# Row-halved scores and outer products, gate weights applied off TensorE, and written-out orders in a fused linear-attention and expert-attention kernel

## The chip, the cores and the metric

The kernel runs on one core of one Trainium2 chip. The metric is the device time of one execution in microseconds, the median of several runs. Engines are named as in the profile: PE (TensorE matmul), PEld (its weight loads), DVE (VectorE), ACT (ScalarE), POOL (GpSimd), SP (the queue that issues most transfers).

## The reference

Two layers, one after the other. The first is linear attention with a norm for each head; the second is attention with four experts, of which each token takes two.

```python
q, k, v: (8, 8, 576, 64)                       # batch, heads, tokens, head size
kv  = einsum('bhsd,bhse->bhde', k, v)
out = einsum('bhsd,bhde->bhse', q, kv)
x   = out / sqrt(mean(out*out, -1) + 1e-6) * g_norm   # heads side by side: (8, 576, 512)

logits = x @ w_gate                            # 4 experts
w      = softmax over the two largest, 0 for the others
for e in range(4):                             # wq, wk, wv: (4, 512, 64)
    q, k, v = x @ wq[e], x @ wk[e], x @ wv[e]
    a   = causal softmax(q @ k.T / 8)
    y  += w[:, e] * (a @ v @ wo[e])            # wo: (4, 64, 512)
```

## The kernel before

The work is cut by batch (b = 0 to 7) and by blocks of 128 tokens (i = 0 to 4, the last has 64). For a batch the stages are, with the names that the profile shows for their PSUM tiles:

- `kv` (L607, p_kv): for each pair of heads, k transposed times v, f32. Two heads write the two column halves of one PSUM bank. `kvx_copy` puts the result into `kvx` as a block-diagonal matrix: head one in partitions 0 to 63, head two in 64 to 127, zeros elsewhere.
- `kt` and `kg` (L641, L651): kv is transposed on PE and multiplied with the gate weights, which lie block-diagonal in `wg_bd`. The four products a head go beside kv in `kvx` (68 columns a head), so the next stage gives the gate logits as well.
- q transposed: on PE for the first two batches (L625), on DVE for the others (L633).
- `out_mm` (L670, p_out): for each of four pairs of heads one f32 product over all 128 partitions with 136 columns. The profile counts two instructions for each f32 product.
- `sq_act` (ACT), `red` (DVE), then `newton`: eleven small DVE operations on 128 x 40 numbers give one over the root. `xm` (L751, POOL) multiplies; `x_tr` transposes x on PE (L625, p_x).
- gates: `gl`, `lg`, `m8`, `sh` (L776), `ex`, `mk`, `gt`, `den`, `rd`, `gate`, nearly all on DVE.
- `v_mm` (L811), `proj` for q and k (L829), in fp32r, for two pairs of experts (pr = 0, 1).
- `sc` (L858, p_sc): the scores of two experts. k transposed lies in two tiles, one an expert, in which the other expert's 64 partitions are zero. So each product runs over all 128 partitions of q. Its 12 products a pass stream 512, 64, 448, 320, 192 and 64 columns for each of the two experts. `exp` (L872, ACT), `msk` (POOL, the causal triangle), `pv` (L892), then a scale by gate over sum on DVE, `ot` (L936) and `y_mm` (L948), copies and stores.

The order is not that of the loops. `graph` lists every task with its engine, an assumed duration and what it needs; `plan` simulates the engines and takes, at each step, the ready task with the smallest due time, which `urgency` computes from a table. `SWAP` moves single PSUM copies between ACT and DVE. PSUM has two small slots (one bank each) and three large ones (two banks each). Each engine works through its queue strictly in the resulting order.

Loads come in through SP, those of batch 0 in part through ACT's queue: `lg0` issues eight small transfers there (norm and gate weights), before ACT's table load and its first copy. PE's `keep_warm` issues nothing here, since `WARM` is 0.

Of the kernel before, what the change touches and what calls it, by code (L numbers as in the profile page):

```python
# [10 lines left out]
FP32 = mybir.dt.float32  # L11
FP32R = mybir.dt.float32r
BF16 = mybir.dt.bfloat16
I32 = mybir.dt.int32
# [3 lines left out]
NB, NCH, EP = 5, 4, 2  # L18
QPE = 2
# [4 lines left out]
LOADS = ("lk", "lv", "lkr", "lvr", "lq", "lg0", "lw", "lwo", "st")  # L24

SWAP = {
    "ws": (('q', 0), ('v', 0),), "qc": ((0, 4), (1, 0), (1, 1), (1, 3),),
    "oc": ((0, 0), (0, 1), (1, 2), (1, 3), (1, 4), (6, 1), (6, 2), (6, 3), (7, 2), (7, 3),),  # L30
    "xc": ((0, 0), (0, 1), (1, 0), (1, 2), (1, 4), (6, 0), (6, 2), (6, 3), (7, 2), (7, 4),),
    "vc": ((0, 0), (6, 0), (6, 1), (6, 2),), "qpc": ((0, 0), (1, 0), (7, 0), (7, 1),),
    "kpc": ((0, 0), (6, 0), (7, 0),), "otc": ((0, 1), (1, 0), (1, 1), (6, 0), (6, 1),),
    "yc": ((0, 1), (0, 4), (1, 0), (1, 1), (1, 2), (1, 3), (1, 4), (6, 2), (6, 3),), "kvx": ((1,), (6,), (7,),),
    "kvc": ((1,),), "ktc": ((7,),),
}


def swapped(n):
    return n[1:] in SWAP.get(n[0], ())  # L40


def earlier(n, m):

    return len(n) > 1 and isinstance(n[1], int) and n[1] < m[1]


def graph(B):
    t = {}

    def add(name, eng, hold, lat, needs=(), tiles=()):
        t[name] = (eng, hold, lat, [n for n in needs if n in t], list(tiles))

    def pe(name, hold, needs, tiles=()):
        add(name, "PE", hold, hold + 0.27, needs, tiles)

    def act(name, took, needs, tiles=()):
        add(name, "ACT", took - 0.10, took + 0.06, needs, tiles)

    def dve(name, took, needs, tiles=()):  # L60
        add(name, "DVE", took - 0.05, took + 0.05, needs, tiles)

    def pool(name, took, needs, tiles=()):
        add(name, "POOL", took - 0.03, took + 0.10, needs, tiles)

    def copy(name, on_act, on_dve, needs, tiles=(), first=dve):

        ways = ((dve, on_dve), (act, on_act))
        if first is act:
            ways = ways[::-1]  # L70
        make, took = ways[swapped(name)]
        make(name, took, needs, tiles)

    R5, R4, R2 = range(NB), range(NCH), range(EP)
    for b in range(B):

        q2 = "ACT" if b == 0 else "SP"
        for p in R4 if b == 0 else R2:
            lat = 0.92 if b == 0 else 1.84
            add(("lk", b, p), "SP", 0.55, lat, (), (("k", b),))  # L80
            add(("lv", b, p), q2, 0.55, lat, (), (("v", b),))
        add(("lkr", b), "SP", 0.65, 0.67, [("kv", b - 2, c) for c in R4])
        add(("lvr", b), q2, 0.65, 0.67, [("kv", b - 2, c) for c in R4])
        for i in R5 if b < QPE else range(8):
            lat = (1.32 if i < NF else 0.66) if b < QPE else 1.06
            add(("lq", b, i), q2 if i % 2 else "SP", 0.6, lat, (), (("q", b),))
        if b == 0:
            add(("lg0",), "ACT", LG0, 0.3)
            dve(("wg",), 0.85, [("lg0",)])
            for nm in "qkv":  # L90
                for p in R2:
                    add(("lw", nm, p), "SP", 0.55, 0.92, (), (("x", nm, p),))
                    name, nd = ("ws", nm, p), [("lw", nm, p), ("lg0",)]
                    (dve if swapped(name) else pool)(name, 0.60 if swapped(name) else 1.08, nd, (("x", nm, p),))
            for p in R2:
                add(("lwo", "o", p), "SP", 0.55, 0.84, (), (("y", "wo", p),))
                dve(("wo", "o", p), 0.42, [("lwo", "o", p)], (("y", "wo", p),))

        for c in R4:
            pieces = (c,) if b == 0 else (c // 2,) if b < QPE else R2  # L100
            nd = [(m, b, p) for m in ("lk", "lv") for p in pieces] + [("lkr", b), ("lvr", b)]
            pe(("kv", b, c), 0.76, nd, (("sm", "kv", b), ("k", b), ("v", b)))
        copy(("kvx", b), 0.76, 0.84, [("kv", b, c) for c in R4] + [("out", b - 2, i) for i in R5], (("sm", "kv", b),))
        copy(("kvc", b), 0.37, 0.43, [("kvx", b), ("kt", b - 2)], (("sm", "kv", b),), act)
        for i in R5:
            if b < QPE:
                last = i == NF
                pe(("q", b, i), 0.38 if last else 0.44, [("lq", b, i)], (("sm", "q", b, i), ("q", b)))
                copy(
                    ("qc", b, i), 0.37 if last else 0.59, 0.42 if last else 0.69, [("q", b, i), ("out", b - 1, i), ("out", b - 1, NF)],  # L110
                    (("sm", "q", b, i),),
                )
            elif i < NCH:
                nd = [("lq", b, i // 2 * 4 + r) for r in R4] + [("out", b - 1, j) for j in R5]
                dve(("qc", b, i), 0.80, nd, (("q", b),))
        pe(("kt", b), 0.20, [("kvc", b)], (("sm", "kt", b),))
        copy(("ktc", b), 0.37, 0.42, [("kt", b)], (("sm", "kt", b), ("kvT", b)))
        pe(("kg", b), 0.42, [("ktc", b), ("wg",)], (("sm", "kg", b), ("kvT", b)))
        copy(("kgc", b), 0.44, 0.34, [("kg", b)] + [("out", b - 2, i) for i in R5], (("sm", "kg", b),))
        for i in R5:  # L120
            pe(
                ("out", b, i), 0.95, [("qc", b, j) for j in ((i, 0) if b < QPE else R4)] + [("kvx", b), ("kgc", b)],
                (("bg", "out", b, i),),
            )
            copy(
                ("oc", b, i), 0.66, 0.73, [("out", b, i), ("xm", b - 1, i), ("gl", b - 1), ("sq", b - 1, i)],
                (("bg", "out", b, i),),
            )
            n = NB * b + i - 3
            act(("sq", b, i), 0.60, [("oc", b, i), ("red", n // NB, n % NB)])  # L130
            dve(("red", b, i), 0.69, [("sq", b, i), ("nw", b - 2, 10)])
        for j in range(11):
            dve(("nw", b, j), 0.19, [("red", b, i) for i in R5] if j == 0 else [("nw", b, j - 1)])
        dve(("gl", b), 0.33, [("nw", b, 10)], (("gl", b),))
        dve(("lg", b), 0.43, [("gl", b), ("mk", b - 2), ("sh", b - 2)], (("gl", b),))
        for i in R5:
            pool(("xm", b, i), 1.08, [("nw", b, 10)], (("x", b, i),))
        for i in R5:
            last = i == NF
            pe(("x", b, i), 0.38 if last else 0.44, [("xm", b, i)], (("sm", "x", b, i), ("x", b, i)))  # L140
# [72 lines left out]
    return t  # L213


NF = 4
LG0 = 5.0
WARM = 0.0
COLD = 6.005
# [787 lines left out]
```

The softmax here doesn't subtract the row's maximum and nothing guards it: scores larger than these inputs give would overflow.

## Time and profile before

| what | value |
|---|---|
| time, median of 3 runs | 254.58 us (253.85 to 255.46) |
| profiled execution, first to last instruction | 250.9 us |
| PE, PEld busy | 221.2 us (88%), 199.0 us (79%) |
| DVE busy | 180.0 us (72%), 510 instructions |
| ACT busy | 148.8 us (59%), 258 instructions |
| POOL busy | 81.1 us (32%), 159 instructions |
| moved by DMA | 40.28 MB, mean 161 GB/s |

The span is that of one execution. The median of the runs lies 3.7 us above it; that part is outside the first and the last instruction. Busy time is a union: two overlapping instructions of an engine count once, so the sum of the durations of a group is larger than what it adds to busy time. Matmuls overlap most. PE's pace is therefore read from the chain of waits, in which each step is counted from the end of the one before, and not from the mean duration of an instruction. Most starving is at both ends: PE is busy 3.79 us between 10 and 20 us, and 20.46 of the last 25.90 us.

### The profile page before, as it was taken

What the parts mean: (1) busy time and instruction counts of PE and PEld (TensorE: products, weight loads), DVE (VectorE), ACT (ScalarE), POOL (GpSimd) and SP (SyncE); (2) the same over time, 40 slices, a digit from 0 to 9 for tenths busy, and PEclk for the clock granted to TensorE, in tenths of its full rate; (3) what the DMA queues carried; (4) which work ended last, traced back from release to release, by engine and by line L of the source; (5) the groups of instructions that cost most, each with busy time, mean ns of one, the idle gap of its engine ahead of it and who ended that gap; (6) DMA issues with size and microseconds to landing.
All of it is one profiled execution on the core that took longest, in us unless ns stands there. A gap on an engine that the chain in (4) does not pass through costs nothing.

```text
span 250.9 us, 6366 instructions
## 1 busy us (share of the span) xinstructions
PE 221.2 (88%) x2456; PEld 199.0 (79%) x2456; DVE 180.0 (72%) x510; ACT 148.8 (59%) x258; POOL 81.1 (32%) x159
## 2 busy tenths in 40 slices
PE   0726957999999999999999998989999699999982
PEld 0714847999999879996998988979988699888850
DVE  0084698688898978998699928976878887794560
ACT  0003450664923976359738993488899556838973
POOL 8300016604800256006700920066006600902310
PEclk9999995999999999999999999999999899999998
DMA  6997999999999989895999993021034100104245
GB/s 172 302 163 223 288 243 283 231 135 285 189 161 332 136 165 343 120 240 184 247 129 272 220 167 103 3 86 42 3 123 173 42 0 3 43 3 146 79 156 189
DMA packets 99433, 40.28 MB, mean 161 GB/s; under 512 B 76618, under 2 KB 94538, under 8 KB 99402
## 3 DMA queue, kind: packets, MB, share of 16 engines
q1 hardware_dynamic: 94320, 38.15, 65.8%
q10 hardware_dynamic: 5082, 1.72, 3.2%
q8 instruction: 19, 0.31, 0.6%
q14 instruction: 12, 0.10, 0.2%
HBM read 30.43 MB, written 9.44 MB: 159 GB/s over the span
## 4 chain that ended last, share of the span: by engine, by line
PE 71%; DVE 11%; DMA 7%; ACT 7%; issue 1%; SPq 1%; ACTq 0%; DVEq 0%
PE p_out L670 13%; PE p_sc L858 9%; PE p_v L811 8%; PE p_k L829 7%; PE p_q L829 7%; PE p_kv L607 6%; PE p_x L625 6%; PE p_y L948 6%; PE p_pv L892 6%; DMA q_b<-in_q_dram 3%; ACT PT L872 3%; DMA k_b<-in_k_dram 3%; DVE sh L776 2%; PE p_q L625 2%; PE p_ot L936 1%
## 5 line engine op out<-in xcount | busy, mean ns | idle before, releaser
L878 POOL TENSOR_SCALAR_AFFINE_SELECT PT<-PT 128x256 bf16<-128x256 bf16 (+1 forms) x80 | 29.0, 383 | 102.0 <-ACT PT L872 87.0
L751 POOL TENSOR_TENSOR x_tok<-o_sb,rs 128x512 f32<-128x512 f32 (+1 forms) x40 | 41.6, 1121 | 54.0 <-DVE rs L725 51.5
L872 ACT ACTIVATE PT<-p_sc 128x128 bf16<-128x128 f32 (+1 forms) x64 | 51.4, 849 | 6.9 <-PE p_sc L858 6.5
L670 PE MATMUL p_out<-kvx,qT 128*128 128x136 f32 x320 | 44.8, 290 | 0.7 <-DVE kvx L493 0.5
L670 PEld LDWEIGHTS p_out<-kvx,qT 128*128 128x128 f32 x320 | 41.9, 199 | 1.4 <-DVE kvx L493 0.5
L858 PE MATMUL p_sc<-qTp,kT 128*128 128x64 f32 (+4 forms) x192 | 39.8, 335 | 0.6 <-ACT PT L872 0.4
L690 ACT ACTIVATE sq<-o_sb 128x512 f32<-128x512 f32 (+1 forms) x40 | 25.3, 637 | 19.2 <-DVE o_sb L493 16.8
L858 PEld LDWEIGHTS p_sc<-qTp,kT 128*128 128x128 f32 x192 | 28.5, 190 | 4.4 <-ACT PT L872 1.1
L696 DVE TENSOR_REDUCE ms<-sq 128x8 f32<-128x520 f32 (+1 forms) x40 | 27.2, 682 | 5.8 <-ACT sq L690 5.5
L493 DVE COPY o_sb<-p_out 128x544 f32<-128x544 f32 (+1 forms) x30 | 21.6, 719 | 13.3 <-PE p_out L670 12.8
L607 PE MATMUL p_kv<-v_b,k_b 128*64 128x64 f32 x512 | 21.7, 236 | 7.6 <-DMA k_b<-in_k_dram 7.5
L811 PE MATMUL p_v<-wv_r,xT 128*128 128x256 f32 x160 | 26.6, 296 | 0.9 <-DVE vext L493 0.7
L625 PE MATMUL p_x<-ident_f,x_tok 128*128 128x128 f32 (+1 forms) x160 | 23.4, 279 | 3.9 <-DVE mk L785 2.2
L607 PEld LDWEIGHTS p_kv<-v_b,k_b 128*64 128x64 f32 x512 | 19.3, 148 | 9.4 <-DMA v_b<-in_v_dram 7.3
L948 PE MATMUL p_y<-wo_b,OT 128*128 128x512 bf16 x80 | 22.7, 381 | 1.0 <-ACT xT L491 0.7
L811 PEld LDWEIGHTS p_v<-wv_r,xT 128*128 128x128 f32 x160 | 21.6, 189 | 2.2 <-DVE vext L493 1.0
L625 PEld LDWEIGHTS p_x<-ident_f,x_tok 128*128 128x128 f32 (+1 forms) x160 | 17.9, 146 | 6.2 <-issue 3.2
L491 ACT CAST xT<-p_x 128x512 fp32r<-128x512 f32 (+1 forms) x30 | 15.7, 546 | 10.6 <-PE p_x L625 10.5
L829 PE MATMUL p_k<-xT,wk_r 128*128 128x288 f32 x128 | 20.2, 301 | 0.0
L491 ACT COPY y<-p_y 128x512 f32<-128x512 f32 (+1 forms) x31 | 17.8, 593 | 3.8 <-PE p_y L948 2.6
L829 PE MATMUL p_q<-xT,wq_r 128*128 128x288 f32 x128 | 19.1, 299 | 0.0
L491 ACT CAST kT<-p_k 64x576 fp32r<-64x576 f32 x26 | 16.5, 634 | 4.2 <-PE p_k L829 4.0
(89 smaller groups left out, 325.1 us busy)
## 6 DMA issues: line engine op xcount, KB each, us to landing
out_dram<-y SPq DMA_DIRECT2D x32, 256.0 KB, 2.2
k_b<-in_k_dram SPq DMA_DIRECT2D x14, 512.0 KB, 5.5
v_b<-in_v_dram SPq DMA_DIRECT2D x14, 512.0 KB, 7.1
q_b<-in_q_dram SPq DMA_DIRECT2D x48, 144.0 KB, 4.8
q_b<-in_q_dram SPq DMA_DIRECT2D x6, 256.0 KB, 8.2
k_rem<-in_k_dram SPq DMA_DIRECT2D x8, 128.0 KB, 3.9
v_b<-in_v_dram ACTq DMA_DIRECT2D x4, 256.0 KB, 6.5
k_b<-in_k_dram SPq DMA_DIRECT2D x4, 256.0 KB, 6.3
```

The source lines that it names most:

```text
L491: nc.scalar.copy(dst, src)
L607: nc.tensor.matmul(p_kv[hh * Dh : (hh + 1) * Dh, c, :], lhsT=lhs, rhs=rhs, start=(j == 0), stop=(j == NF), skip_group_check=True,)
L625: nc.tensor.transpose(p_t[:, c, :nt], chunk(c)[:nt], ident_f[:nt, :nt])
L670: nc.tensor.matmul(p_o[:, c // 2, (c % 2) * 256 : (c % 2) * 256 + 2 * GW], lhsT=blocks_of(qT, c)[:, i * P : (i + 1) * P], rhs=kvx[b % 2][: ...
L696: nc.vector.tensor_reduce(mss[b % 2][:nt, i, :], sqs[(NB * b + i) % 3][:nt], axis=AX_X, op=AluOpType.add)
L751: nc.gpsimd.tensor_tensor(out=buf(("x", b, i), [P, NCH, P], FP32, "x_tok")[:nt].rearrange("p c (h r) -> p h r c", h=H), in0=ob[:nt, i, :, ...
L811: nc.tensor.matmul(p_v[:], lhsT=blocks_of(xTs[b % 2], c)[:, i * P : (i + 1) * P], rhs=w_r["v"][:, c, :, :].rearrange("p e f -> p (e f)"), ...
L829: nc.tensor.matmul(p_p[:, s, 0:HALF], lhsT=w_r[nm][:, c, 2 * pr : 2 * pr + 2, :].rearrange("p e f -> p (e f)"), rhs=blocks_of(xTs[b % 2], ...
L858: nc.tensor.matmul(p_s[:, el, o : o + hi - lo], lhsT=kTs[pr][el][:, kb * P : (kb + 1) * P], rhs=tiles["qTp", b, pr][:, lo:hi], start=True, ...
L872: nc.scalar.activation(PT[:, :, d0 : d0 + o], big("sc", b, pr, j)[:, :, 0:o], ACTF.Exp, scale=scale)
L878: nc.gpsimd.affine_select(out=d, in_=d, compare_op=AluOpType.is_ge, fill=0.0, base=0, pattern=[[0, 2], [1, w]], channel_multiplier=-1,)
L948: nc.tensor.matmul(p_y[:], lhsT=blocks_of(OTs[b % 2], pr)[:, qc * P : (qc + 1) * P], rhs=wo_b[:, pr, :], start=(pr == 0), stop=(pr == EP - 1),
```

## The change

All tasks stay, but for `kt`, `kg` and their copies. What differs:

- **Row halves.** `sc` and `out_mm` now take one head's or expert's 64 partitions on each side. Head 0 uses partitions 0 to 63, head 1 the others, into two PSUM banks, in alternating instructions. The zero-filled k tiles and the block-diagonal `kvx` are gone; k transposed is copied in one piece.
- **Gate weights off PE.** kv is copied to `kvx`, multiplied with spread-out gate weights (`kvg_mul`, DVE or POOL) and summed (`kvg_sum`, DVE).
- **Gate weights spread by PE.** At the start two rows of gate weights are loaded through POOL's queue, and `gb` multiplies them with a row of ones, which puts them on all partitions.
- **Norms.** ACT's Ln and Exp give a first value and three small operations refine it. In batch 0 each block of tokens is normed by itself.
- **Zero matmuls.** PE runs products of zeros ahead of five tasks, 30 of them ahead of `gb`.
- **Orders.** `graph` and `plan` are gone. The order of all tasks, the engine of each elementwise task and the slot of each buffer are written out as strings. 30 of the 40 `xm` products go to DVE, 22 of the 40 squares to POOL. PSUM is four slots of two banks, of which small tiles take halves.
- x is turned by an fp32r product with an identity, and not by a transpose. The last 64-token block of y is computed and stored in two column halves. q loads of the first two batches are split in two and all issued by SP.

```diff
+ZEROS = {
+    ("gb",): 30, ("q", 0, 0): 1, ("q", 0, 2): 2, ("out", 0, 3): 4, ("v", 0, 0): 3,
+}
...
     def lv(b, p):
         load_main(queue(b, True), v_t(b), v, b, p)
+        if (b, p) == (0, NCH - 1):
+            nc.scalar.preload_act_table_set("natural_log_exp_and_others")
...
-    def lg0():
-        nc.scalar.dma_start(g_wide[:], g_norm.unsqueeze(0).to_broadcast([P // Dh, Dh]))
...
+    def gb():
+        p_w = big("gb")
+        for a in range(2):
             for m in range(EP):
-                nc.scalar.dma_start(wg_st[pp, m], by_head[:, 4 * m + 2 * c2 : 4 * m + 2 * c2 + 2, :])
...
+                nc.tensor.matmul(
+                    p_w[a * Dh : (a + 1) * Dh, m, :], lhsT=one_row[0:1, :], rhs=wg_row[a][:, m * 512 : (m + 1) * 512],
+                    start=True, stop=True, skip_group_check=True,
+                )
...
+    def kvg_mul(b, g):
+        ms = of_part(b, g)
+        n = ms.stop - ms.start
+        ew(("kgm", b, g)).tensor_tensor(
+            out=kvgs[b % 2][:].rearrange("p e (m k) d -> p e m (k d)", k=2)[:, :, ms],
+            in0=kvx[b % 2][:, ms, E : E + 2 * Dh].unsqueeze(1).to_broadcast([P, E, n, 2 * Dh]),
+            in1=wg_t[:].rearrange("p e (m k) d -> p e m (k d)", k=2)[:, :, ms], op=AluOpType.mult,
+        )
...
+    def kvg_sum(b, g):
+        ms = of_part(b, g)
+        nc.vector.tensor_reduce(
+            gates_of(kvx[b % 2])[:, ms], kvgs[b % 2][:].rearrange("p e (m k) d -> p m k e d", k=2)[:, ms], axis=AX_X,
+            op=AluOpType.add,
+        )
...
     def out_mm(b, i):
-        p_o = big("out", b, i)
+        p_o, nt = big("out", b, i), blocks[i][1]
         for c in range(NCH):
-            nc.tensor.matmul(
-                p_o[:, c // 2, (c % 2) * 256 : (c % 2) * 256 + 2 * GW],
-                lhsT=blocks_of(qT, c)[:, i * P : (i + 1) * P],
-                rhs=kvx[b % 2][:, c, :, :].rearrange("p a g -> p (a g)"),
-                start=True,
-                stop=True,
-            )
+            for hh in range(2):
+                pp = slice(hh * Dh, (hh + 1) * Dh)
+                nc.tensor.matmul(
+                    p_o[:nt, hh, c * GW : (c + 1) * GW],
+                    lhsT=qTs[b % NQT][pp, c * S + i * P : c * S + i * P + nt],
+                    rhs=kvx[b % 2][pp, c // 2, c % 2 * GW : (c % 2 + 1) * GW],
+                    start=True,
+                    stop=True,
+                )
...
+    def ln(b, g):
+        cols, ms = span(b, g), mss[b % 2][:].rearrange("p n h -> p (n h)")
+        nc.scalar.activation(roots[b % 2][:, cols], ms[:, cols], ACTF.Ln)
+
+    def rs(b, g):
+        cols = span(b, g)
+        nc.scalar.activation(rstds[b % 2][:, cols], roots[b % 2][:, cols], ACTF.Exp, scale=-0.5)
...
     def xm(b, i):
...
-        nc.gpsimd.tensor_tensor(
...
+        ew(("xm", b, i)).tensor_tensor(
...
+    def x_tr(b, i):
+        p_t, nt = small("x", b, i), blocks[i][1]
+        for c in range(NCH):
+            nc.tensor.matmul(
+                p_t[:, c * P : c * P + nt], lhsT=tiles["x", b, i][:, c, :], rhs=ident_r[:, 0:nt], start=True, stop=True
+            )
...
             for el in range(2):
+                pp = slice(el * Hd, (el + 1) * Hd)
                 nc.tensor.matmul(
                     p_s[:, el, o : o + hi - lo],
-                    lhsT=kTs[pr][el][:, kb * P : (kb + 1) * P],
-                    rhs=tiles["qTp", b, pr][:, lo:hi],
+                    lhsT=kTs[(2 * b + pr) % 3][pp, kb * P : (kb + 1) * P],
+                    rhs=tiles["qTp", b, pr][pp, lo:hi],
...
     with tc.manual_schedule():
-        for t, _, n in plan(tasks, POOLS, {n: urgency(n) for n in tasks})[0]:
...
+        for n in order:
+            if n in ZEROS:
+                zero_matmuls(n, ZEROS[n])
             emit[n[0]](*n[1:])
```

## The prediction

> **What bounds the kernel now.** I read the windows by stage first, then the chain of waits, the groups and the wait list. In the windows each engine's busy time stands with its instruction count:
>
> ```profile
> 10.00:20.00 10.00, 3.79 (x44) 3.07 (x44) 5.50 (x13) 1.37 (x2) 0.00 (x0) 1.00 1.03 173
> ...
> 50.00:75.00 25.00, 25.00 (x325) 23.67 (x327) 21.39 (x64) 13.72 (x24) 9.32 (x16) 1.00 1.12 193
> ...
> 175.00:200.00 25.00, 22.84 (x208) 20.16 (x207) 19.94 (x51) 21.50 (x39) 8.61 (x15) 0.97 0.24 86
> ```
>
> Columns: window, length, busy us of PE, PEld, DVE, ACT, POOL, clock, DMA share, GB/s. See three stages: a start of 50 us in which PE starves; 175 us (50 to 225) with PE busy 170.1 us by the sum of the seven windows, 97%; a tail of 26 us. DVE has 142.4 us in the middle, 81%: it is the next limit, not far below. The chain agrees and names the lines:
>
> ```profile
> PE 71%; DVE 11%; DMA 7%; ACT 7%; issue 1%; SPq 1%; ACTq 0%; DVEq 0%
> PE p_out L670 13%; PE p_sc L858 9%; PE p_v L811 8%; PE p_k L829 7%; PE p_q L829 7%; PE p_kv L607 6%; PE p_x L625 6%; PE p_y L948 6%; PE p_pv L892 6%; DMA q_b<-in_q_dram 3%; ACT PT L872 3%; DMA k_b<-in_k_dram 3%; DVE sh L776 2%; PE p_q L625 2%; PE p_ot L936 1%
> ```
>
> PE's pace, first from the chain in order of time, then from the timelines of PE and of the weight loads (start, us, what):
>
> ```profile
> 130.33 0.93 PE p_out L670 x8
> ...
> 132.92 2.48 PE p_kv L607 x80
> ...
> 236.15 1.37 PE p_sc L858 x10
> ```
>
> ```profile
> 131.62 1.30 PE L829 MATMUL p_k<-xT,wk_r 128*128 128x288 f32 x8
> 132.85 0.69 PE L607 MATMUL p_kv<-v_b,k_b 128*64 128x64 f32 x16
> ...
> 139.25 0.54 PEld L651 LDWEIGHTS p_kg<-wg_bd,kvT 128*128 128x128 f32 x4
> ...
> 139.59 0.19 PEld L651 LDWEIGHTS p_kg<-wg_bd,kvT 128*128 128x128 f32 x1
> ```
>
> The kg matmuls stream only 16 columns, yet their loads start (139.59 - 139.25)/3 = 0.113 us apart: a full f32 load takes that long. The kv instructions load 64 columns and write alternate column halves; 2.48/80 = 0.031 us each is about half of 0.113/2, so two halves work at once. And k's eight, at 1.06/8 = 0.132, would let the next begin at 132.68; kv begins at 132.85, so entering the halved mode cost 0.17.
>
> The start and the stalls, from the wait list, the chain and a group:
>
> ```profile
> ACT L428 <- DMA wg_st<-in_moe_w_gate_dram: 18.6, 1, 18.6
> ...
> PEld p_q L625 <- ACT kvc L491: 5.8, 1, 5.8
> ```
>
> ```profile
> 10.06 7.89 DMA q_b<-in_q_dram
> ...
> 193.06 3.93 DVE sh L776
> ```
>
> ```profile
> L751 POOL TENSOR_TENSOR x_tok<-o_sb,rs 128x512 f32<-128x512 f32 (+1 forms) x40 | 41.6, 1121 | 54.0 <-DVE rs L725 51.5
> ```
>
> ACT issues eight gate-weight and norm loads up to 19.5 us; its first copy (kvc) comes after them, and PE waits. The sh line is a 20-element subtraction that took 3.93 us while POOL ran five x_tok products.
>
> [...]
>
> **PE, part by part.** Pair prices are the larger of a load (0.113) and a stream (0.46 ns a column from 0.119 for v's 256).
> - Scores: now 12 a pass, ten at 1.37 and the two of 512 at 0.22 (y's 0.88/4), 1.81 us. Afterwards six pairs: 64, 64 and 192 columns at 0.113, then 0.147, 0.206 and 0.22: 0.91. Sixteen passes: 29.0 to 14.6, **-14.4**.
> - out: 8 instructions of 0.116 (0.93) become 16 with a load each; two at a time 16 x 0.113/2 = 0.90, and half for the 64-token tile. 40 x 0.93 = 37.2 becomes 32 x 0.90 + 8 x 0.45 = 32.4: **-4.8**.
> - kt and kg off PE: six loads of 0.113 a batch, 0.68 x 8: **-5.4**. Last y block in column halves: 8 x 0.22: **-1.8**.
> - x by fp32r product instead of transpose: load-bound on both sides (0.105 now): 0. [...]
> - Mode changes: the PE order has 72 stretches of one mode against 20: 52 x 0.17 = **+8.8** (0 to 15).
>
> Sum -17.6 of 203 (now kv 19.8, q 4.3, kt and kg 5.4, out 37.2, x 17, v 19, k and q 34, scores 29, pv 15.4, ot 4.4, y 17.6), so 25.4 us a batch becomes 23.2. These edits are charged wholly to PE, which is the path; about 0.85 of them, -15, fall in the middle stage.
>
> **DVE, ACT, POOL, queues.** DVE, by rows of before: Newton 17.5 out, 26 small operations of 0.2 in: -12.3. Thirty x_tok products come from POOL at 0.67 (the weight product L584): +20.1. kv times gate weights: products 5 x 1.2 + 2 x 0.67, sums 7 x 1.25 + 2 x 0.68 (scaled from 0.685 for 520), less 10.1 of kvx, kvT and kvc copies: +7.5. Most of sh, and parts of gt, gl, gate and inv go to POOL: -15. PSUM copies exchanged with ACT: -5; set-up 0. About -5 on 202 summed: DVE stays near 177 busy while the span shrinks. ACT loses 22 squares (0.64) and the doubled kT copies (26 to 9), gains 24 Ln/Exp (0.24) and vext copies: about -17, off the path. POOL trades 30 x 1.12 for 22 squares of about 1.1 and small work: even. What POOL blocks on DVE is the unknown: 30 products, each meeting half a POOL operation in 0.4 of cases, 0.2 us: +6, from 0 to 15. That puts DVE's share of a middle of 160 us at 144/160, 90%. At 81% PE lost 4.9 us; I take 6 more (0 to 12) as given back. What is late next is a copy out of PSUM behind a product in DVE's queue, and PE waits for that bank. sh's own stalls on the chain (3.9 and 1.7) mostly go: -4. SP issues ten more q loads and eight more stores at 0.6 us, and two q loads that were ACT's; the middle hides them behind data that arrives batches early. In the start they stand before the weight loads. POOL issues four gate and norm loads ahead of its memsets, not on the path.
>
> **The start.** PE first runs 30 zero matmuls, then gb, with kv queued behind both. Zeros: kv's first sixteen took 1.12 us against 0.64 later, so cold is 0.22 x 1.75 = 0.39; [...] 8 us from 1.3 to 9.4. gb: four f32 products of 512 columns, 0.88 each scaled from out: to 12.9. kv warm, 2.5: to 15.4, against 12.9 now. That is 2.5 late. But ACT is free, so copy, product and sum of both parts (2 x 1.6, begun at 14.4) release out(0) at about 17.7, against 26.2 now. Each tile is then normed alone: square, sum, Ln, Exp, three steps and product are about 3.5 us, and ACT's square and copy (1.25 a tile) pace the rest: v(0) ends near 33 against 52.9. Before had by then done kv(1), q(1) and out(1) too, 2.5 + 2.2 + 4.6 = 9.3. Gain 52.9 - 33 - 9.3 = 10.6. Low end 4: the q load landed at 17.95 and may again; high end 14.
>
> **Sum.** Start -10.5; middle -15 for PE, +6 given back to DVE, -4 for sh; tail -1 (the last store chain stays). -24.5 on a span of 250.9 gives 226.4. The median (254.58) lies 3.7 above the profiled span; I add that to every span: **230 us**. Own range 217 to 243.
>
> **Rivals.** (1) DVE takes the bound: 177 + 15 of locks, kept at 90% as an in-order queue, is 213; with 18 us of idle start and 5 of tail, 236 + 3.7 = 240; range 236 to 250. For: 81% already. Against: the worst lock of before leaves. (2) Row halves don't overlap, the slower side: out 32 x 1.81 + 8 x 0.90 = 65.1 (+27.9), scores still 29.0, less 7.2, plus 8.8: PE +29; less 11.5 for start and tail, 272. It decides from where PE grows by 12: the sum is -17.6 + 47.1 g, g the share of pairs that run singly, so g above 0.63. For: only columns are seen overlapping. Against: kv's 0.031. (3) The start is held by data: DMA share is 1.0 up to 150 us, so only 4 of the 10.5 come, and half of the middle's 13: about 243. (4) Overlap without mode cost, and DVE keeping up: 210 to 217.
>
> **Chances.** Forecast 0.63, rivals (1) and (3) together 0.22, (2) 0.07, (4) 0.08. The range takes the forecast, most of (1) and (3) and part of (4): 213 to 246. A measurement here tells about 1% from no change. Faster by over 1%: the forecast, (4) and nearly all of (1) and (3): 0.90; within 1%: 0.04; slower: 0.06.
>
> **What would show it.** Right: sixteen out instructions near 0.9 us, a score pass near 0.9; first out near 18 us, v(0) done near 33; DVE at 80% or more of the span; sh no longer in the chain; one table load. Wrong: out tiles of 1.7 us; a start of 45 us; DVE leading the chain; xm on DVE well over 0.67.

## The result, and the profile after

The changed kernel takes 277.23 us (median of 4 runs, 275.66 to 278.55); the kernel before, run beside it, 254.44 (253.85 to 255.46). The ratio is 1.0909, 95% interval 1.0834 to 1.0984: slower by 9%, where 230 was forecast. The profiled execution took 278.12, with a span of 276.3 and a mean granted clock of 0.873; before it was 250.9 and 0.977. From here on a measured time is the median of the executions within 1.5% of the fastest of their kernel, as in the ratios, and the range is that of all; the expectations quote medians of all.

Windows by stage of the changed kernel (window, length, busy us of PE, PEld, DVE, ACT, POOL, clock, DMA share, GB/s):

```profile
25.00:50.00 25.00, 22.39 (x175) 19.41 (x175) 13.42 (x36) 7.74 (x23) 4.74 (x7) 0.59 0.94 234
50.00:75.00 25.00, 21.20 (x280) 18.94 (x280) 19.91 (x38) 13.06 (x25) 9.70 (x16) 0.89 0.98 184
...
125.00:150.00 25.00, 24.13 (x254) 21.55 (x255) 18.10 (x37) 11.75 (x20) 9.69 (x16) 0.75 0.63 145
...
200.00:225.00 25.00, 21.16 (x253) 18.82 (x250) 19.53 (x36) 12.96 (x23) 13.48 (x20) 0.82 0.14 49
```

Two things are new. PE has gaps (21.20 of 25 where it had 25.00), and the clock column is low in windows where PE is busy: from 25 to 50 only 0.59. In the page's slices the clock row shows how long such spells last; first the row of before (a slice is 6.3 us), then that of the changed kernel (6.9 us):

```profile
PEclk9999995999999999999999999999999899999998
```

```profile
PEclk9998557999599779995599999995999669889998
```

The page's chain of waits, by engine and by line:

```profile
PE 58%; DVE 25%; ACT 4%; issue 4%; DMA 4%; SPq 2%; POOL 0%; ACTq 0%; DVEq 0%; POOLq 0%
PE p L427 10%; PE p L574 10%; PE p L593 9%; DVE x_tok L508 9%; PE p L519 6%; PE p L712 5%; PE p L744 5%; PE p L654 4%; PE p L377 3%; PE p L620 3%; DVE ms L456 2%; DMA q_b<-in_q_dram 2%; DVE xT L270 2%; DMA out_dram<-y 1%; DVE qT L417 1%
```

DVE went from 11% of a span of 251 to 25% of one of 276, from some 28 to 69 us, and about 24 of these (8.5% before rounding) are one line: x_tok (L508), the norm's product. Its group, and the waits that it ends:

```profile
L508 DVE TENSOR_TENSOR x_tok<-o_sb,rstd 128x512 fp32r<-128x512 f32 x30 | 35.5, 1265 | 0.1
```

```profile
PE p L519 <- DVE x_tok L508: 10.5, 12, 2.1
...
PEld p L519 <- DVE x_tok L508: 8.9, 10, 2.3
```

The chain in order of time (start, us, what) shows the clock in single pieces:

```profile
36.67 2.86 PE p L574 x12
...
53.81 1.99 PE p L427 x32
...
71.17 2.93 PE p L574 x12
```

Twelve matmuls of v take 2.86 and 2.93 with the clock column at 0.50 in both stretches; at the pace of before (0.95 for eight) they are 1.43. Two row-halved out tiles, with the column at 1.00, take 1.99, where two whole ones of before took 1.86.

### The profile page after: what moved, and what is told of

The parts are those of the page before. It is cut to its first block, busy times and chain, and to the rows that moved or that the text cites. A ratio compares the mean times of both kernels' runs of the same rounds, so it can differ in the third digit from the quotient of the medians.

```text
span 276.3 us, 6932 instructions
## 1 busy us (share of the span) xinstructions
PE 239.8 (87%) x2792; PEld 202.5 (73%) x2792; DVE 191.3 (69%) x425; ACT 132.2 (48%) x247; POOL 98.5 (36%) x182
## 4 chain that ended last, share of the span: by engine, by line
PE 58%; DVE 25%; ACT 4%; issue 4%; DMA 4%; SPq 2%; POOL 0%; ACTq 0%; DVEq 0%; POOLq 0%
PE p L427 10%; PE p L574 10%; PE p L593 9%; DVE x_tok L508 9%; PE p L519 6%; PE p L712 5%; PE p L744 5%; PE p L654 4%; PE p L377 3%; PE p L620 3%; DVE ms L456 2%; DMA q_b<-in_q_dram 2%; DVE xT L270 2%; DMA out_dram<-y 1%; DVE qT L417 1%
## 5 line engine op out<-in xcount | busy, mean ns | idle before, releaser
L634 ACT ACTIVATE PT<-p 128x1024 bf16<-128x1024 f32 (+1 forms) x64 | 50.8, 840 | 8.0 <-PE p L620 7.6
L427 PE MATMUL p<-kvx,qT 64*128 64x68 f32 (+1 forms) x640 | 40.7, 274 | 3.5 <-DVE o_sb L270 3.4
L427 PEld LDWEIGHTS p<-kvx,qT 64*128 64x128 f32 (+1 forms) x640 | 37.4, 186 | 8.4 <-DVE o_sb L270 3.7
L519 PE MATMUL p<-ident_r,x_tok 128*128 128x128 f32 (+1 forms) x160 | 30.8, 338 | 12.5 <-DVE x_tok L508 10.5
L519 PEld LDWEIGHTS p<-ident_r,x_tok 128*128 128x128 f32 x160 | 27.7, 252 | 16.1 <-DVE x_tok L508 8.9
L574 PE MATMUL p<-wv_r,xT 128*128 128x256 f32 x160 | 35.7, 380 | 1.0 <-ACT xT L268 0.6
L508 DVE TENSOR_TENSOR x_tok<-o_sb,rstd 128x512 fp32r<-128x512 f32 x30 | 35.5, 1265 | 0.1
L574 PEld LDWEIGHTS p<-wv_r,xT 128*128 128x128 f32 x160 | 30.2, 271 | 3.8 <-DVE xT L270 1.1
L452 POOL TENSOR_TENSOR sq<-o_sb 128x512 f32<-128x512 f32 (+1 forms) x22 | 22.7, 1037 | 19.5 <-DVE o_sb L270 11.3
L620 PE MATMUL p<-qTp,kT 64*128 64x64 f32 (+4 forms) x192 | 24.1, 354 | 1.2 <-ACT qTp L268 0.4
## 6 DMA issues: line engine op xcount, KB each, us to landing
out_dram<-y SPq DMA_DIRECT2D x32, 256.0 KB, 2.9
k_b<-in_k_dram SPq DMA_DIRECT2D x4, 256.0 KB, 6.7
v_b<-in_v_dram ACTq DMA_DIRECT2D x4, 256.0 KB, 8.6
```

The source lines that it names most:

```text
L427: nc.tensor.matmul(p_o[:nt, hh, c * GW : (c + 1) * GW], lhsT=qTs[b % NQT][pp, c * S + i * P : c * S + i * P + nt], rhs=kvx[b % 2][pp, c // ...
L508: ew(("xm", b, i)).tensor_tensor(out=buf(("x", b, i), [P, NCH, P], FP32R, "x_tok")[:].rearrange("p c (m k r) -> p m k r c", m=NCH, k=2), i ...
L519: nc.tensor.matmul(p_t[:, c * P : c * P + nt], lhsT=tiles["x", b, i][:, c, :], rhs=ident_r[:, 0:nt], start=True, stop=True)
L574: nc.tensor.matmul(p_v[:, 0 : E * Hd], lhsT=blocks_of(xTs[b % 2], c)[:, i * P : (i + 1) * P], rhs=w_r["v"][:, c, :, :].rearrange("p e f -> ...
L620: nc.tensor.matmul(p_s[:, el, o : o + hi - lo], lhsT=kTs[(2 * b + pr) % 3][pp, kb * P : (kb + 1) * P], rhs=tiles["qTp", b, pr][pp, lo:hi], ...
L634: nc.scalar.activation(PT[:, :, d0 : d0 + o], big("sc", b, pr, j)[:, :, 0:o], ACTF.Exp, scale=scale)
```

## The experiments

**What the x_tok products cost on DVE.** In the timeline of the changed kernel, DVE's products and POOL's instructions beside them (start, us, engine, line):

```profile
62.90 3.79 DVE L508 TENSOR_TENSOR x_tok<-o_sb,rstd 128x512 fp32r<-128x512 f32 x4
...
66.11 2.69 POOL L395 TENSOR_TENSOR kvg<-kvx,wg_t 128x1024 f32<-128x1024 f32 x1 [3.47 <-ACT kvx L268]
...
68.91 1.02 DVE L508 TENSOR_TENSOR x_tok<-o_sb,rstd 128x512 fp32r<-128x512 f32 x1
...
179.82 4.94 DVE L508 TENSOR_TENSOR x_tok<-o_sb,rstd 128x512 fp32r<-128x512 f32 x4
...
179.94 1.84 POOL L508 TENSOR_TENSOR x_tok<-o_sb,rstd 128x512 fp32r<-128x512 f32 x1 [0.21 <-DVE rstd L487]
...
181.65 1.17 POOL L493 TENSOR_TENSOR gl<-o_sb,rstd 128x160 f32<-128x160 f32 x1
```

Four products take 3.79 while POOL is idle but for the last 0.6, some 0.95 each, and 4.94 while POOL works. Between the first four and the fifth DVE has a `gl` of 2.45 beside POOL's kvg, where the other two on DVE took 0.33, and the fifth begins at 68.91, just after kvg's end at 68.80. Such stretches of DVE beside POOL are what the prediction and the expectations call locks; that the one waits for the other is a reading of these times. So the products were moved back to POOL, alone (in `unpack`):

```diff
+    engine.update({n: "G" for n in ns if n[0] == "xm"})
```

> The changed kernel with all 40 x_tok products on POOL. Theory A (thirty products on DVE, 1.02 to 2.16 us each, 35.5 us in all, keep DVE from its copies): DVE busy falls by some 30 us to 160, the time to 255 to 268 us. Theory B (what counts is how late x is, not who computes it: five products in a row on POOL are 5.7 us, against about 4.5 shared): no gain, 275 to 290 us.

Measured: 261.98, 262.51 and 263.89 in three executions and 257.87 in a fourth, against 254.97 before: 13 to 19 of the 22 are gone. The chain of waits by engine and the group of products, of the execution of 262.51:

```profile
PE 64%; DVE 16%; POOL 8%; ACT 5%; issue 4%; DMA 1%; ACTq 0%; DVEq 0%; POOLq 0%
...
L509 POOL TENSOR_TENSOR x_tok<-o_sb,rstd 128x512 fp32r<-128x512 f32 x40 | 42.8, 1132 | 10.9 <-ACT xT L269 6.6
```

POOL's product is no faster (1132 ns), but DVE, now 160.0 busy for 191.3, is free for the copies out of PSUM. The placement of this one step is the largest single cost that was found. How it costs is shown only in part: the clock is higher too, 0.911 against 0.873, and the shorter waits and the better clock were not taken apart.

**The clock.** The same was asked from the other side: three zero matmuls ahead of every x tile of batches 1 to 7, nothing else changed.

```diff
+ZEROS.update({("x", b, i): 3 for b in range(1, 8) for i in range(5)})
```

> The changed kernel with three zero matmuls ahead of each x tile of batches 1 to 7 (105 of 0.22 us, 23 us of PE work that waits for nothing but its PSUM slot). Theory C (PE's waits at x let the granted clock fall to half, and the work after it runs at half pace): mean clock from 0.87 to 0.95 or more, 255 to 268 us, although no wait is removed. If the waits alone are the cost and the clock is a by-product: 277 to 295 us.

Measured: 271.63 (270.1 to 272.54), ratio 1.0676 (1.0613 to 1.0740), clock 0.966. The clock came back as theory C said, the time hardly: it lies between the two forecasts. On the chain of waits the zero matmuls (105 new ones beside 40) grew from 5% to 9% of the span, some 10 us, so they took part of what they restored; and DVE still held 29% of it.

Next, with the products on POOL, the squares went to ACT, where before has them all; then, each on top of that, out in whole-array products, or six zeros ahead of only the first x tile of a batch. The whole-array version leaves out the zeros of the block-diagonal matrix, so it sums two heads and serves for its time alone.

```diff
+    engine.update({n: "G" if n[0] == "xm" else "A" for n in ns if n[0] in ("xm", "sq")})
```

> The changed kernel with all 40 x_tok products on POOL and all 40 squares on ACT, as the kernel before has them. Theory A (the assignment of the norm's steps to engines costs the time: locks between DVE and POOL, and a loaded POOL): POOL falls from 118 busy to about 96, ACT rises from 132 to about 146, and the time falls from 262 (products on POOL alone) to 252-258. Theory C (what is left over is the clock, fed by an order with little cover behind each x tile): 259-264, the clock stays near 0.91. Theory M (what is left over is the row-halved out product): 259-264 too, and out stays the chain's first line.

Measured: 262.98 (262.36 to 267.15), ratio 1.0290 (1.0216 to 1.0364). The profiled execution took 267.15 with a clock of 0.904; the two fastest had 0.933 and 0.920. No gain over the run before shows, though POOL's busy time fell from 118.4 to 96.8.

```diff
-            for hh in range(2):
-                pp = slice(hh * Dh, (hh + 1) * Dh)
...
+            nc.tensor.matmul(
+                p_o[:nt, c // 2, c % 2 * 2 * GW : (c % 2 + 1) * 2 * GW],
+                lhsT=qTs[b % NQT][:, c * S + i * P : c * S + i * P + nt],
+                rhs=kvx[b % 2][:, c // 2, :],
```

> As the run with products on POOL and squares on ACT, but out is computed in whole-array products, four of 128 rows and 136 columns a tile in place of eight of 64 rows and 68 columns; both heads of a column block are summed instead of kept apart, as the block-diagonal zeros of the kernel before are left out. Theory M (row halves in out are dear beside whole-array work, as the +19 of the kernel before with out in row halves says): 8 to 18 below its partner. Theory A (row halves work at 0.83 a tile against 0.93, and only placement and waits matter): within 3 of its partner, or up to 4 slower.

Measured: 255.96 (254.52 to 260.5), ratio 1.0044 (1.0007 to 1.0081): 7.0 below its partner, just under the 8 to 18 of theory M and more than theory A allowed. The page's clock rows hint how. First the partner with row halves (its execution of 267.15), then whole-array out:

```profile
PEclk9999559999799989997799799995899959999995
```

```profile
PEclk9999999998699979999999999999999999999998
```

The mean is 0.904 in one and 0.977 in the other; over the executions that the medians are taken from it is 0.920 to 0.933 against 0.976 to 0.983. PE's waits at x_tok are the same in both pages (8.3 and 8.1 by the wait lists of the weight loads), so it is not the waits that differ, but what they do to the clock.

```diff
+ZEROS.update({("x", b, 0): 6 for b in range(1, 8)})
```

> As the run with products on POOL and squares on ACT, with six zero matmuls ahead of the first x tile of batches 1 to 7 (42 in all, 9 us if none falls into a wait). Theory C (the clock, lost after PE's waits at x): clock over 0.95 and 3 to 8 below its partner. Theory A: clock up, time within 2 of its partner or above it, as the waits themselves stay.

Measured: 258.36 (257.86 to 265.06), ratio 1.0113 (1.0045 to 1.0180), clock 0.98. So zeros give 4.6, and whole-array out 7.0. Both together:

> The run with whole-array out (256.1; both heads of a block summed) with six zero matmuls ahead of the first x tile of batches 1 to 7. If whole-array out helped only by keeping the clock (0.977 there), zeros add nothing: 255-259. If the modes themselves cost, both gains add (9 and 6.5): 248-252.

Measured: 258.72 (257.92 to 259.73), ratio 1.0104 (1.0051 to 1.0158), clock 0.986: nothing more. With the clock held by the same zeros, row-halved out (258.36) and whole-array out (258.72) take the same time. So whole-array out helped through the clock; the price of the modes themselves does not show on top.

One more idea was that the chain from out to x is long because its small steps hop to POOL. All of them went to DVE:

```diff
+    engine.update({n: "V" for n in ns if n[0] in ("nb", "gl", "sh", "gt", "gate", "iv")})
```

> The run with products on POOL, squares on ACT and zeros ahead of the first x tiles (258.5), with the small products of the norm and the gate (the middle Newton step, gl, sh, gt, gate, inv) all on DVE instead of 30 or so of them on POOL. Theory H (hops to a POOL that has masks and products ahead of them lengthen the chain from out to x): 252-256. Theory N (they are off the path, or DVE's locks take as much): 257-260.

Measured: 264.23 (262.99 to 268.23), ratio 1.0306 (1.0247 to 1.0364), 5.9 above its partner. The gain of theory H did not come. Whether small work on POOL is right is not shown, for the clock differs as well. The partner's row first, then this run's:

```profile
PEclk9999999998899999999999999999999769999999
```

```profile
PEclk9998555999999999999999999999999999999997
```

By the means (0.98 of 256.1 and 0.956 of 262.8) this run spent 13 us more at half clock, mostly in its start. That is up to 6.5 us of work, as much as the whole difference.

**TensorE alone.** Two runs have no kernel around PE: rows of tiles, mixtures, and bursts after waits of known length.

> Nothing of the kernel is computed; the output is zeros. TensorE alone runs, in a row: 30 zero matmuls; 24 out tiles of four whole-array f32 products (128 rows, 136 columns); 24 out tiles of eight row-halved products (64 rows, 68 columns); 16 times four fp32r products of 256 columns (as v) and a whole tile; 16 times the same and a row-halved tile; then bursts of ten whole tiles, with waits for 1, 2, 3 and 5 DVE copies of 544 columns between them, and the same with row-halved tiles. Theory M (an entry into row halves costs, a row-halved tile does not): 0.93 a whole tile and 0.83 a row-halved one in the rows of 24; in the mixed rows a pair with row halves takes 0.2 to 0.4 longer than a pair without. Theory A (no such cost): the mixed rows differ by less than 0.1 a pair. Theory C (the clock falls after waits): half clock after the waits of 3 and 5 copies (2.2 and 3.6), full clock after 1. Theory R (row-halved work counts as less activity): half clock after shorter waits, or without any, in the row-halved stretches only.

The timeline of PE in this run (L55 is whole-array out, L67 row-halved out, L75 four matmuls as in v):

```profile
9.41 22.40 PE L55 MATMUL p<-g,qs 128*128 128x136 f32 x192
31.74 21.66 PE L67 MATMUL p<-g,qs 64*128 64x68 f32 x384
...
74.35 0.72 PE L75 MATMUL p<-qr 128*128 128x256 f32 x4
74.91 1.09 PE L55 MATMUL p<-g,qs 128*128 128x136 f32 x8
75.75 0.72 PE L75 MATMUL p<-qr 128*128 128x256 f32 x4
...
77.44 0.73 PE L75 MATMUL p<-qr 128*128 128x256 f32 x4
78.11 1.11 PE L67 MATMUL p<-g,qs 64*128 64x68 f32 x16
79.15 0.73 PE L75 MATMUL p<-qr 128*128 128x256 f32 x4
...
124.77 9.53 PE L55 MATMUL p<-g,qs 128*128 128x136 f32 x80 [1.71 <-DVE g L82]
136.78 11.20 PE L55 MATMUL p<-g,qs 128*128 128x136 f32 x80 [2.47 <-DVE g L82]
151.97 17.34 PE L67 MATMUL p<-g,qs 64*128 64x68 f32 x160 [3.99 <-DVE g L82]
```

In a row, a whole tile takes 22.40/24 = 0.93 and a row-halved one 21.66/24 = 0.90. Among v's matmuls a pair with a whole tile takes 75.75 - 74.35 = 1.40, one with row halves 79.15 - 77.44 = 1.71. So 0.03 is gained in the tile and 0.34 lost in entering and leaving the row halves, 0.17 for each change of mode on average: a lone row-halved tile costs 0.31 more than a whole one. The last three lines are bursts of ten tiles after a wait: whole ones after 1.71 run at full pace, after 2.47 they lose 1.67 (some 3.4 us at half clock, then full); row-halved ones after 3.99 take 17.34, about half pace to the very end, and the next three bursts, after waits of 0.96 to 2.48, do so too. No expectation had quite this: row-halved out does not bring the clock back.

> Nothing of the kernel is computed; the output is zeros. TensorE alone: three times twelve whole-array out tiles, a wait (1, 2, 3 DVE copies) and ten row-halved out tiles; then, each after twelve whole tiles and a wait of five copies (4.0, after which the clock was at half before): eight pairs of v and a row-halved tile; twenty v; twenty-four row-halved score pairs of 512 columns; sixteen column-halved groups as in kv; fifty zero matmuls; ten row-halved out tiles. Theory R (row-halved products keep a full clock but do not bring it back): row-halved out and score rows stay at half clock to their end, whole-array v and zeros return to full in 3 to 4, the mixed row late or not at all. Theory T (the clock returns after a fixed time, and the first run's bursts were a coincidence of their waits): all return in 3 to 4. After the waits of 1 and 2 copies the row-halved rows run at full clock by both.

The timeline of PE (L67 row-halved out, L75 v, L89 score rows of 512 columns, L97 column halves as in kv, L105 zeros; each burst but the first follows a wait of 4.0):

```profile
43.84 15.66 PE L67 MATMUL p<-g,qs 64*128 64x68 f32 x160 [1.71 <-DVE g L82]
...
130.49 1.98 PE L67 MATMUL p<-g,qs 64*128 64x68 f32 x16
...
150.68 11.33 PE L75 MATMUL p<-qr 128*128 128x256 f32 x80
...
177.85 7.81 PE L89 MATMUL p<-qr 64*128 64x512 f32 x48
...
201.68 9.70 PE L97 MATMUL p<-ks,qs 128*64 128x64 f32 x256
...
255.43 17.34 PE L67 MATMUL p<-g,qs 64*128 64x68 f32 x160
```

After a wait of only 1.71 the row-halved burst takes 15.66, where one after a wait of 0.95 took 9.15: it starts at full clock, loses it 1.9 us in, and does not regain it. The row of v and row-halved tiles by turns is still at half pace in its last pair, 24 us after the wait (1.98 for a tile). The clock column of windows of 5 us says when the clock changes (0.57 of 5 us is 0.7 us at full clock and 4.3 at half):

```profile
45.00:50.00 5.00, 5.00 (x58) 5.00 (x57) 0.00 (x0) 0.00 (x0) 0.57 0.00 0
...
60.00:65.00 5.00, 5.00 (x34) 5.00 (x33) 0.00 (x0) 0.00 (x0) 0.72 0.00 0
...
75.00:80.00 5.00, 5.00 (x60) 5.00 (x62) 0.00 (x0) 0.00 (x0) 0.65 0.00 0
...
90.00:95.00 5.00, 5.00 (x34) 4.88 (x33) 0.00 (x0) 0.00 (x0) 0.65 0.00 0
```

Between changes the column reads 1.00 or 0.50. So the clock fell at 45.7, rose at 62.8, fell at 76.5 and rose at 93.5, which is 5, 4 and 5 times some 3.41 us apart; all sixteen changes of this trace lie on that grid. What counted in these two runs, then, was not the length of a wait alone but how much of it fell between two points of the grid. From 144.7 to 148.1 it was 1.67 us beside whole-array work, and the clock stayed; 2.3 us or more took it. From 42.3 to 45.7 it was 1.52 us beside row-halved out, and the clock fell (one case each). Once lost, it came back at the end of the first such stretch that was filled, or nearly, with v, score rows, column halves, zeros or whole tiles: 4.3 us into v, 4.4 into score rows, 4.5 into column halves, 2.8 into zeros, which differ only in where the work began on the grid. Stretches filled with row-halved out never brought it back. Theory R holds, with one correction: not rows as such, but these short f32 products in row halves. Why them is open: the score rows, which do bring it back, differ in columns (512 against 68) and in type (fp32r against f32).

**Row halves in the kernel before.** Its order is fixed by its own planned costs, which were left as they were.

```diff
-                    lhsT=kTs[pr][el][:, kb * P : (kb + 1) * P],
-                    rhs=tiles["qTp", b, pr][:, lo:hi],
+                    lhsT=kTs[pr][el][el * Hd : (el + 1) * Hd, kb * P : (kb + 1) * P],
+                    rhs=tiles["qTp", b, pr][el * Hd : (el + 1) * Hd, lo:hi],
```

> The kernel before with row-halved scores alone (each expert's 64 partitions of both operands), same order. Theory R (halves run two at a time, 1.81 to about 0.9 us a pass): 240 to 247 us. Theory D (entering and leaving the halved mode among whole-array work eats it, 0.17 us and more at each of some 100 changes): 250 to 258 us.

Measured: 252.26 (248.97 to 255.97, 20 runs), ratio 0.9863 (0.9825 to 0.9902). The cut was to take 14.4 off PE. It took 3.5 off the time by the ratio, and 2.0 by the medians of all executions (252.98 against 254.97). The page's chain of waits, of an execution of 255.06:

```profile
PE 64%; DVE 14%; ACT 10%; DMA 7%; issue 3%; ACTq 1%; DVEq 0%
```

PE's share fell from 71 to 64%, DVE and ACT rose: what PE no longer did, it mostly waited.

> The kernel before with row-halved scores and row-halved out products, same order. Theory R: 0.93 to about 0.85 us for an out tile on top, 236 to 245 us, 2 to 4 below the kernel with row-halved scores alone. Theory D: out's sixteen instructions and more mode changes cost what they save, the same as or slower than scores alone.

This adds out in row halves, edited as in the change. Measured: 272.10 (271.55 to 279.18), ratio 1.0679 (1.0620 to 1.0738), clock 0.904: some 20 worse than scores alone. In the changed kernel the same part cost 7. Both signs of the runs on TensorE alone are there: a lone tile of 1.04 in the chain, and spells of half clock, as the clock row shows:

```profile
PEclk9977578556999999999999999999999658999999
```

How much of the 20 is the clock and how much the tiles was not taken apart in this kernel.

> The kernel before with row-halved scores (253.0 alone) and the gate-weight and norm loads issued by POOL instead of ACT. If the start waits for ACT's queue (its first copy came after eight loads, and PE waited 5.8 for it), 246-250. If the start is held by data that the DMA engines move anyway (their share is 1.0), 251-255.

With the gate-weight loads issued by POOL as well (`nc.scalar.dma_start` becomes `nc.gpsimd.dma_start` in `lg0`): 252.4 (250.26 to 253.9), ratio 0.9870 (0.9791 to 0.9948), the same as scores alone. The 5.8 us wait for ACT's queue was no gain to be had. The chain of this run, an execution of 251.09, has PE lower still:

```profile
PE 60%; DVE 16%; ACT 9%; DMA 5%; SPq 4%; issue 2%; POOL 2%; DVEq 0%; ACTq 0%
```

**Good parts, new order.** The kernel before plans its own order from costs and priorities. It was given row-halved scores with their costs, one copy of kT, Ln and Exp with one refinement, and the gate loads on POOL's queue; out, squares and products stay as before.

> The kernel before with four parts of the change: row-halved scores, one copy of kT for both heads in place of two padded ones, Ln/Exp norms with one Newton step, gate-weight loads off ACT's queue; its planner is given the new costs and its priorities are searched anew (planned end 235.6 against 243.6). out stays whole-array, squares on ACT, products on POOL. Theory P (the saved PE time of row-halved scores was lost because order and priorities were made for the old costs): 244-249, below both kernels. Theory B (the kernel before is bound by the chain through DVE and ACT as much as by PE): 250-254, as row-halved scores alone.

Measured: 243.66 (243.31 to 245.26), ratio 0.9535 (0.9478 to 0.9592), below both kernels. The same parts in the old priorities:

> The same parts as the replanned kernel (243.7), with the planner's new costs but the kernel before's own priorities (planned end 246.5 against 235.6). Theory P (the order brought the gain): 251-258. Theory Q (the parts bring it whatever the order): 243-248.

Measured: 250.51 (249.08 to 251.44), ratio 0.9842 (0.9775 to 0.9909), no more than scores alone gave. And the new search without row-halved scores:

> Control: the kernel before with Ln/Exp norms and gate loads off ACT's queue, but scores whole-array with two padded copies of kT as before; priorities searched anew with the same effort (planned end 244.1). If the row-halved scores pay once the order fits them: 250-254 here, so some 8 between the two. If any new search gains: 243-247.

Measured: 243.95 (242.55 to 245.47), ratio 0.9590 (0.9518 to 0.9662), where 250 to 254 was to show that the scores pay. So the new search was worth more than the scores. To price the scores in a good order, they were swapped into this one, instruction for instruction, together with the single copy of kT that they allow:

> The replanned control without row-halved scores (243.95), its order kept instruction for instruction, with row-halved scores and one copy of kT in place of two padded ones. If PE's time is the bound in this order, the scores' saving shows (11.4 by the pitches of the two replanned kernels): 233-238. If the order alone decides, as in the kernel before (253.0 of 255): 241-244.

Measured: 241.72 (240.3 to 243.18, 6 runs), ratio 0.9449 (0.9399 to 0.9499): 1.5% under the control by the ratios to before (0.9% by the two medians, which were not measured side by side), about the 1.4% in the kernel before. The busy times of the control, then of this run, from their pages:

```profile
PE 215.0 (89%) x2456; PEld 194.2 (81%) x2456; DVE 167.7 (70%) x445; ACT 151.9 (63%) x274; POOL 86.6 (36%) x167
```

```profile
PE 212.3 (88%) x2443; PEld 184.2 (76%) x2456; DVE 156.1 (65%) x435; ACT 144.2 (60%) x262; POOL 86.9 (36%) x167
```

PE's busy time falls by 2.7, that of the weight loads by 10. It is the second that shows what became free. DVE and ACT are busy for 11.6 and 7.7 less, with the single copy of kT, so the 1.5% is at most what the scores are worth here.

> The same parts, with the planner told the new costs and its priorities searched on from those of the control (planned end 236.0). If the first replanned kernel lost its saving to an unlucky start: 234-240. If not: 242-246, as both before.

Measured: 240.46 (240.09 to 242.0, 6 runs), ratio 0.9410 (0.9362 to 0.9457): the lowest median of the study, though its interval overlaps that of the run before it. Its windows from 50 to 100 us:

```profile
50.00:75.00 25.00, 25.00 (x321) 22.51 (x321) 19.60 (x54) 16.12 (x29) 10.18 (x16) 1.00 0.85 166
75.00:100.00 25.00, 24.83 (x345) 21.61 (x341) 20.91 (x54) 17.02 (x33) 8.66 (x15) 1.00 1.00 248
```

PE is full again and the clock is 1.00 there, with row-halved scores in it.

> The replanned kernel (243.7; its clock was 0.79 between 25 and 50 us) with the planner's own zero matmuls turned on in PE's planned gaps up to 45 us. If the clock there holds the start: 240-243. If zeros stand in the way of work that comes early: 244-247.

Measured: 245.93 (245.36 to 246.59), ratio 0.9662 (0.9592 to 0.9732), clock 1.00: zeros in the start hold the clock and cost some 2 us against the same kernel without them (243.66).

## Why the prediction was wrong

The sum was -15 for PE in the middle (-17.6 in all stages), +6 given back to DVE, -4 for sh, -10.5 for the start and -1 for the tail: -24.5. Two of its steps turned the gain into a loss: what thirty x_tok products on DVE cost, which was priced too low, and the granted clock, which is no term of it at all. Two more terms returned next to nothing of what was forecast: PE's cut and the start. A rough estimate from the runs, in which the parts overlap: 7 to 13 for the products beyond the 6 allowed, 7 for out and its clock, 10 for the start, 12 or 13 for PE's cut, 3 for sh, some 39 to 46 of the 47 between 230 and 277. Point by point:

- **Row halves overlap: the time was right.** A row-halved out tile in a row took 0.90, the number forecast: sixteen instructions of 64 rows in the time of eight of 128 (0.93). That each of the sixteen needs a full load of 0.113, so that two must run at once, was the author's assumption; it was not shown by itself. 0.17 for a change of mode held in the runs on TensorE alone, though it had been read from column halves. In the changed kernel's chain a tile takes 1.0. A score pass, forecast at 0.91, took 22.1/16 = 1.38 from its starts to those of the work after it in the first replanned kernel, against 33.5/16 = 2.09 in the control: 11.4 saved. Entries into the mode fall on the matmul before (v's four took 0.65 ahead of row halves and 0.56 ahead of a whole tile), 39 groups x 0.09 = 3.5, so about 8 net. So the scores' cut was sized too large (14.4). Rival (2) was false; that its 272 came closest to the 277 measured was luck.
- **"These edits are charged wholly to PE, which is the path": a step that failed.** About 8 of PE's time returned 2 to 3.5, in the old order and in a better one. The reading behind it was PE busy for 97% of the middle. A matmul's record is about 300 ns (out's of before 290 in the mean) while the next starts 116 ns later, so a gap of up to some 0.2 us counts as busy. The weight loads showed more of what became free: from the control to its partner with row-halved scores their busy time fell by 10, that of matmuls by 2.7. Before, the loads were busy for 156.7 of the 175 us of the middle, 90%: this points at slack of a tenth, in which waits for copies and products hid, but was not measured by itself.
- **"Thirty x_tok products come from POOL at 0.67", and 0.2 of locks each: mis-sized, and charged to the wrong place: the step that cost most.** The row taken was a product with the same size, another layout and another second operand. They measured 1.09 in the median and 1.27 in the mean: 35.5 and not 20.1 + 6. With the products on POOL 13 to 19 us came back, more than the difference of 9.4, for x stands next in PE's order: PE waited 10.5 us for DVE's products, in 12 waits, and the clock improved with them. DVE's total was forecast at 177 and was 191; "90% as an in-order queue" was rival (1), with 240. It named the mechanism and underpriced it; the sum had put it at 6 (0 to 12).
- **The granted clock: not in the sum at all.** As the clock column reads 1.00 or 0.50 between changes (second run on TensorE alone), (1 - 0.873) x 276.3 x 2 = 70 us passed at half clock, against 12 before. Waits at x_tok of up to 2.3 stand before four of its eight spells; the first and longest, from 25 to 45 us, began in a wait of 2.12 for q transposed. Whole-array out gave 7.0 back and zeros 4.6, and both 4.3, so this is one cost. The prediction allowed for slow zero matmuls at the very start (8 us for the thirty, an estimate; they took 8.2 in the changed kernel) and did not ask what a wait would do later. Idle time of less than a step of the grid found here, 3.41, was enough: the clock fell after waits of 2.47 ahead of whole-array work and of 1.71 ahead of row-halved out.
- **out -4.8, modes +8.8: right for TensorE, the wrong sign in the kernel.** The price of a change of mode stands, but the part was worth +7 in one kernel and some +20 in the other; in the changed kernel this went through the clock, which the sum left out.
- **The start: -10.5, measured about 0.** The first out came at 18.1 (forecast 17.7; before 26.2). But the exponential of the first gate softmax came at 42 against 39 before, and at 37 with whole-array out and a full clock. The clock fell at 25 and stayed at half until 45: sixteen of the twenty matmuls of v(0), the x tiles and kv(1) ran in it, and the last four of v(0), forecast to end near 33, came at 50.7. Of the lead of 8 at the first out, 2 to 3 are left even without that. Where the rest goes in the tile-by-tile norm was not tried.
- **sh, -4: mostly not there.** One sh of 2.75 us still stands on the chain, at 128.9, beside a POOL product (`kvg`) of 2.36, as the 3.93 of before stood beside five POOL products; the other sh on DVE took 0.18. That it waits for POOL is a reading of these times.

Together: products on POOL and squares on ACT bring 277.2 to 263.0, and whole-array out, through the clock, to 256.0, which is about the time of before. The first of these steps went in part through the clock too: its profiled execution spent (1 - 0.904) x 265.3 x 2 = 51 us at half clock, against 70. That the remaining parts are worth nothing there, while row-halved scores are worth 1.4% elsewhere, is not settled. The waits for x_tok of POOL that are left (8.1 on the weight loads) point at an order with little between out and x; the order of the changed kernel is written out and was not planned anew, so this was only argued.

## What to carry to other kernels

Read how near PE is to its bound from the weight loads and from the starts of matmuls, not from busy PE (here the loads fell by 10 where busy PE fell by 2.7); and before moving a step to a faster engine, look at who waits for it, and in whose queue it will stand. Use row halves where the columns are many (scores: a pass of 1.38 against 2.09 in the two replanned kernels) and keep them together; short f32 products in row halves, scattered among whole-array work, cost two changes of mode a tile (0.17 each) and did not bring a fallen clock back (ten tiles took 17.34 to the end of the burst, where 9.15 is full pace). After a change of costs, plan the order anew: new priorities were worth 3% here with the same parts (243.66 against 250.51), about twice what these parts gave in the old order. The kernel before was not searched anew with its old costs, so how much of this the search alone would have found is open.

## What was unexpected of the hardware

- In the second run on TensorE alone all sixteen changes of the clock lie on a grid of some 3.41 us, whatever work ran: it fell at 45.7, 76.5 and 107.2 us and rose at 62.8, 93.5 and 137.9.
- After a wait of 4.0 us, whole-array f32 work regained the full clock in about 3 us in the one case measured (10.96 for ten tiles against 9.53); row-halved 68-column f32 products never did: 17.34 for ten tiles in each burst, four bursts in a row, and also in turns with v, for 24 us.
- The same products kept a full clock when no wait came before: 21.66 for 24 tiles, with the page's clock row at 9.
- A wait of 1.71 was harmless ahead of whole-array tiles and cost the clock ahead of row-halved ones, in one case each. Where a wait fell on the grid counted too: the harmless one was split by it into 1.14 and 0.57, but 1.67 in one piece was harmless as well, and 1.52 ahead of row-halved tiles was not.
- A DVE product of 128 x 512 took 0.67 into the weights' layout, in two cases, and never less than 1.02 into x_tok's. The second operand differs as well; which of the two it is was not tried.
